# A sigmoid-attention and GELU feed-forward kernel: sixteen SBUF tiles made 32 bytes longer each

## The chip, the cores and the metric

The kernel runs on one core of one Trainium2 chip. The metric is the device time of one execution in microseconds; the time of a version is the median of its runs. TensorE (PE) does the matrix products, ScalarE (ACT) the activations and casts, VectorE (DVE) the subtractions, GpSimd (POOL) a few products early on, SyncE (SP) issues most DMAs. SBUF is the on-chip memory of 128 partitions; an address here is a byte offset within a partition, the same on all partitions of a tile.

## What is computed

```python
scores = q @ k.T / sqrt(64) - log(448)          # 8 batches, 12 heads, 448 positions, head_dim 64
x = (sigmoid(scores) @ v) -> [3584 tokens, 768]
h = x @ w_in                                    # [768, 2048]
g = 0.5 * h * (1 + erf(h / sqrt(2)))            # exact GELU
out = g @ w_out                                 # [2048, 768]
```

The weights come as 64-bit floats. Nearly every matrix product is made of products of a rounded high part and of a low rest (names ending in h and l), in the type fp32r.

## The kernel before

**Work.** The tokens of the eight batches are worked in seven feed-forward passes of T = 512 tokens each (448 of one batch and 64 of another). `attention_first` does the attention of the first two batches and decodes the first weights from 64-bit floats. Then for each pass t, `ffn1(t)` computes the hidden layer, and `window(t + 2, t)` does the second layer of pass t (`ffn2`) with the attention of batch t + 2 woven in between, a few matmuls of one, then a few of the other. The order of instructions on every engine is the order in which the program is written (a manual schedule).

**The g tiles.** There are sixteen of them, one for each block fc of 128 hidden features, tags g0 to g15, made by `g_tile` (line 66). Each has 2 x 512 words of 4 bytes: the high part `g[fc][:, 0]` at its start and the low part `g[fc][:, 1]` 2048 bytes further on. During decoding the same sixteen places first hold the decoded `w_in` (`first_w`, made on line 160, filled by POOL on line 163), which `prepare_to` splits into weights for the first pass (lines 237 and 238) and the SP queue stores to a scratch in HBM (line 201). Afterwards `ffn1` writes g into them: ACT writes the high part (line 466), DVE the low part (line 467).

**Who reads g on PE.** In `ffn2` each of 12 weight units (e, half) has 8 blocks, and each block makes three matmuls into `po`:

```python
nc.tensor.matmul(po, wl, g[fc][:, 0], start=first, stop=False)   # L497
nc.tensor.matmul(po, wh, g[fc][:, 1], start=False, stop=False)   # L498
nc.tensor.matmul(po, wh, g[fc][:, 0], start=False, stop=last)    # L499
```

The second operand after the output is the stationary one (128 columns of weights, 512 bytes of a partition), the third is the moving one (512 columns, 2048 bytes). In all that is 7 x 12 x 8 x 3 = 2016 matmuls, 672 on each of the three lines. `ffn1` makes as many into `ph` (lines 450 to 452) with `xh` and `xl` as moving operands.

**Where the tiles lie.** Tiles lie one behind another in the order of the pools and of first use. The weights `hl` (name `whl`) have four places: for unit number i in `prepare_to`, two buffers of the tag `whl` when i % 4 is 0 or 1 (and in the whole first pass), the buffers of the tags `raw` and `me` when i % 4 is 2 or 3. The first unit of every `ffn2` has i % 4 = 0. The table gives start addresses and their remainders mod 512; a slice of weights lies a multiple of 512 bytes from its tile's start, and so does the low part of a g tile.

| tile | address before | mod 512 | address after | mod 512 |
|---|---|---|---|---|
| xh, xl | 16544, 28832 | 160, 160 | the same | 160, 160 |
| g0 | 41120 | 160 | 41120 | 160 |
| g1 | 45216 | 160 | 45248 | 192 |
| g8 | 73888 | 160 | 74144 | 416 |
| g11 | 86176 | 160 | 86528 | 0 |
| g15 | 102560 | 160 | 103040 | 128 |
| whl in tags raw, me | 117408, 126624 | 160, 160 | 117920, 127136 | 160, 160 |
| qs (three buffers) | 143008, 144800, 146592 | 160, 416, 160 | each 512 more | 160, 416, 160 |
| ka, kb (first buffers) | 148384, 154528 | 416, 416 | each 512 more | 416, 416 |
| whl in tag whl | 211360, 219552 | 416, 416 | 211872, 220064 | 416, 416 |

Of the kernel before, what the change touches and what calls it, by code (L numbers as in the profile page):

```python
# [17 lines left out]
P = 128  # L18
# [4 lines left out]
def tile_sigmoid_attention_gelu_ffn(  # L23
# [25 lines left out]
    T = S + TOK  # L49
# [4 lines left out]
    const = ctx.enter_context(tc.tile_pool(name="const", bufs=1))  # L54
# [7 lines left out]
    xh = const.tile([P, NPAIR, T], F32R, name="xh")  # L62
    xl = const.tile([P, NPAIR, T], F32R, name="xl")
    g, first_w = {}, {}

    def g_tile(fc, name, dtype=F32R):
        return const.tile([P, 2, T], dtype, tag=f"g{fc}", name=name)

    scr_in = tc.dram_tile([NF, P, NC * P], F32, name="scr_in")
    scr_out = tc.dram_tile([NO, P, NFH * P], F32, name="scr_out")  # L70
# [21 lines left out]
    def decoder():  # L92
# [57 lines left out]
        def end(i):  # L150
            high = raws.pop(i)[:, :, 1]
            ended[0] += 1
            m, e = parts.pop(i)
            nc.vector.scalar_tensor_tensor(  # L154
                e, high, 0x80000000, e, op0=ALU.bitwise_and, op1=ALU.bitwise_or
            )
            kind, u, c0, w = chunks[i]
            if c0 == 0 and kind == "in":
                first_w[kind, u] = g_tile(u, f"w_in{u}", F32).rearrange("p a b -> p (a b)")
            elif c0 == 0:  # L160
                first_w[kind, u] = sb.tile([P, WU], F32, tag="wst", name=f"w_out{u}", bufs=WST)
            t = first_w[kind, u][:, c0 : c0 + w]
            nc.gpsimd.tensor_tensor(t, m.bitcast(F32), e.bitcast(F32), op=ALU.mult)  # L163
# [291 lines left out]
    def ffn1(b):  # L455
        for fc in range(NF):
            if b == 0:
                W.store_to(fc + 3)
            if (b, fc) not in phs:
                hidden(b, fc, range(NC - 1))  # L460
            W.prepare_to(W.pos[b, "in", fc] + (2 if b == 0 else AHD))
            ph = hidden(b, fc, range(NC - 1, NC))
            g[fc] = g_tile(fc, f"g{b}_{fc}")
            gf = sb.tile([P, T], F32, tag="tmp", name=f"gf{b}_{fc}", bufs=3)
            nc.scalar.activation(gf, ph, AF.Gelu)  # L465
            nc.scalar.activation(g[fc][:, 0], ph, AF.Gelu)  # L466
            nc.vector.tensor_tensor(g[fc][:, 1], gf, g[fc][:, 0], op=ALU.subtract)  # L467
            W.prepare_to(W.pos[b, "in", fc] + (3 if b == 0 else AHD + 1))
            if fc in (NF - 10, NF - 8):
                load_pair(b + 2, (fc - NF + 10) // 2)  # L470
                load_v(b + 2, (fc - NF + 10) // 2)
            if fc in (NF - 4, NF - 2):
                split_head(b + 2, (fc - NF + 4) // 2)
            if fc == NF - 1:
                load_pair(b + 2, 2)
                load_v(b + 2, 2)
            if b == 0:
                W.decode(PACE_A + PACE_F * min(fc + 1, NF - 1) // (NF - 1))
# [101 lines left out]
```

## Time and profile before

| | |
|---|---|
| median of 3 runs (lowest to highest) | 1275.95 us (1274.27 to 1277.11) |
| the profiled execution: time, span of its trace | 1277.24 us, 1275.5 us |
| busy share of the span: PE, ACT, DVE, POOL | 96%, 68%, 65%, 7% |
| granted TensorE clock, mean over the span | 0.991 of full |

Each instruction in the trace has a start and a duration. Matmuls are pipelined: the next one starts before the one ahead of it ends, so that the distance from start to start, not the duration, is what one costs on PE when they follow each other without a wait. "PEld" rows are loads of the stationary operand, which run beside the matmul ahead.

### The profile page before, as it was taken

Reading aid. Unit: us, or ns where it says so; the run is one execution under the profiler, and the core shown is the slowest. Engines: PE = TensorE matmul, PEld = TensorE weight load, DVE = VectorE, ACT = ScalarE, POOL = GpSimd, SP = SyncE. Lnnn points to the kernel's source line nnn. Section 1 sums busy time; section 2 is a strip of 40 time slices with the busy share of each in tenths; the row PEclk is TensorE's granted clock in tenths of the full one; section 3 lists DMA queues with packets and bytes.
Section 4 is the critical chain, followed back from the end, with each engine's and each line's share of the span. In section 5 each row is a group of like instructions: output and inputs, shape, how many; then the busy total and the mean of one; then the engine's idle time right before and its main releaser. Section 6 shows DMA issues by size and latency. Waiting matters only on the chain.

```text
span 1275.5 us, 15676 instructions
## 1 busy us (share of the span) xinstructions
PE 1229.8 (96%) x5448; PEld 985.9 (77%) x5448; DVE 826.7 (65%) x1359; ACT 872.2 (68%) x1427; POOL 89.1 (7%) x84
## 2 busy tenths in 40 slices
PE   7889888989999999999999999999999999999998
PEld 4445665756888888888888888888888888888887
DVE  5776888883458973479844798436985458863420
ACT  7987677764459984499844898547995469964421
POOL 1111333441000000000000000000000000000000
PEclk9999898999999999999999999999999999999999
DMA  7764756652445323554225442254422444323330
GB/s 284 233 213 127 219 185 191 204 183 88 153 143 168 113 67 102 164 158 149 66 84 167 155 143 70 91 159 150 151 75 82 156 154 139 109 66 99 116 123 34
DMA packets 83775, 176.41 MB, mean 138 GB/s; under 512 B 24432, under 2 KB 37744, under 8 KB 83696
## 3 DMA queue, kind: packets, MB, share of 16 engines
q1 hardware_dynamic: 81968, 169.12, 41.8%
q0 software_dynamic: 1728, 6.29, 1.2%
q8 instruction: 43, 0.70, 0.2%
q14 instruction: 36, 0.29, 0.1%
HBM read 149.03 MB, written 26.35 MB: 137 GB/s over the span
## 4 chain that ended last, share of the span: by engine, by line
PE 80%; DVE 7%; ACT 5%; DMA 2%; issue 2%; POOL 2%; SPq 0%; DVEq 0%; POOLq 0%; ACTq 0%
PE po L497 11%; PE po L498 11%; PE po L499 11%; PE ph L450 10%; PE ph L451 10%; PE ph L452 10%; PE pav L398 7%; PE sc L331 4%; PE sc L332 4%; ACT a L355 2%; PE pav L364 2%; POOL w_out L163 2%; DVE me_ring L154 1%; DVE whl L238 1%; DMA scr_in<-w_in 1%
## 5 line engine op out<-in xcount | busy, mean ns | idle before, releaser
L450 PE MATMUL ph<-xh,whl 128*128 128x512 f32 x672 | 263.9, 393 | 10.3 <-DVE whl L238 10.3
L497 PE MATMUL po<-g,whl 128*128 128x512 f32 x672 | 264.0, 393 | 9.5 <-DVE whl L238 9.5
L498 PE MATMUL po<-g,whl 128*128 128x512 f32 x672 | 262.9, 391 | 0.0
L499 PE MATMUL po<-g,whl 128*128 128x512 f32 x672 | 262.8, 391 | 0.0
L451 PE MATMUL ph<-xl,whl 128*128 128x512 f32 x672 | 262.8, 391 | 0.0
L452 PE MATMUL ph<-xh,whl 128*128 128x512 f32 x672 | 262.6, 391 | 0.0
L238 DVE TENSOR_TENSOR whl<-wst,whl 128x768 fp32r<-128x768 f32 (+1 forms) x168 | 179.5, 1072 | 66.8 <-ACT whl L237 63.6
L467 DVE TENSOR_TENSOR g<-gf,g 128x512 fp32r<-128x512 f32 x112 | 77.8, 695 | 213.2 <-ACT g L466 213.2
L465 ACT ACTIVATE gf<-ph 128x512 f32<-128x512 f32 x112 | 66.8, 597 | 205.1 <-PE ph L452 190.9
L450 PEld LDWEIGHTS ph<-xh,whl 128*128 128x128 f32 x672 | 126.9, 189 | 40.3 <-DVE whl L238 13.3
L237 ACT CAST whl<-wst 128x768 fp32r<-128x768 f32 (+1 forms) x168 | 155.4, 928 | 2.2 <-PE po L499 0.8
L497 PEld LDWEIGHTS po<-g,whl 128*128 128x128 f32 x672 | 126.6, 188 | 38.8 <-DVE whl L238 11.6
L355 ACT ACTIVATE a<-sc 128x896 f32<-128x896 f32 x192 | 129.6, 728 | 28.3 <-PE sc L332 24.0
L499 PEld LDWEIGHTS po<-g,whl 128*128 128x128 f32 x672 | 126.6, 188 | 27.1
L452 PEld LDWEIGHTS ph<-xh,whl 128*128 128x128 f32 x672 | 127.0, 189 | 26.6
L451 PEld LDWEIGHTS ph<-xl,whl 128*128 128x128 f32 x672 | 127.0, 189 | 26.2
L498 PEld LDWEIGHTS po<-g,whl 128*128 128x128 f32 x672 | 126.6, 188 | 23.8
L331 PE MATMUL sc<-qs,ka 128*128 128x448 f32 x288 | 108.6, 377 | 14.9 <-ACT a L355 13.6
L348 DVE TENSOR_TENSOR al<-a,ah 128x896 fp32r<-128x896 f32 x120 | 97.8, 854 | 34.8 <-ACT ah L347 34.8
L332 PE MATMUL sc<-qs,kb 128*128 128x448 f32 x288 | 107.4, 373 | 0.0
L293 DVE TENSOR_TENSOR qs<-qr,qs 64x448 fp32r<-64x448 f32 x96 | 62.0, 646 | 45.8 <-ACT qs L292 43.9
L347 ACT CAST ah<-a 128x896 fp32r<-128x896 f32 x120 | 85.6, 753 | 6.1 <-PE pav L398 4.6
(62 smaller groups left out, 1514.6 us busy)
## 6 DMA issues: line engine op xcount, KB each, us to landing
wst<-scr_in SPq DMA_DIRECT2D x96, 384.0 KB, 3.1
wst<-scr_out SPq DMA_DIRECT2D x72, 512.0 KB, 3.2
kr<-k_dram SPq DMA_DIRECT2D x47, 448.0 KB, 4.4
vr<-v_dram SPq DMA_DIRECT2D x48, 256.0 KB, 3.9
qr<-q_dram SPq DMA_DIRECT2D x48, 224.0 KB, 3.2
out_dram<-ob SPq DMA_DIRECT2D x42, 224.0 KB, 2.0
raw<-w_in_dram SPq DMA_DIRECT2D x20, 384.0 KB, 4.2
scr_in<-w_in SPq DMA_DIRECT2D x16, 384.0 KB, 4.3
```

What stands on the lines that cost most here:

```text
L237: nc.scalar.copy(hl[:, 0, :w], t[:, :w])
L238: nc.vector.tensor_tensor(hl[:, 1, :w], t[:, :w], hl[:, 0, :w], op=ALU.subtract)
L331: nc.tensor.matmul(o, ka[:, keys], qs, start=True, stop=False)
L332: nc.tensor.matmul(o, kb[:, keys], qs, start=False, stop=True)
L348: nc.vector.tensor_tensor(al[t][:, c], a[t][:, c], ah[t][:, c], op=ALU.subtract)
L355: nc.scalar.activation(a, sc, AF.Sigmoid, bias=NEG_LOG_S, scale=SCALE)
L450: nc.tensor.matmul(ph, wl, xh[:, cc], start=cc == 0, stop=False)
L451: nc.tensor.matmul(ph, wh, xl[:, cc], start=False, stop=False)
L452: nc.tensor.matmul(ph, wh, xh[:, cc], start=False, stop=cc == NC - 1)
L497: nc.tensor.matmul(po, wl, g[fc][:, 0], start=first, stop=False)
L498: nc.tensor.matmul(po, wh, g[fc][:, 1], start=False, stop=False)
L499: nc.tensor.matmul(po, wh, g[fc][:, 0], start=False, stop=last)
```

## The change

`g_tile` asks for 8 more words (32 bytes) behind the 2 x 512 of each g tile and hands out a view of the first 2 x 512. Nothing reads or writes the added words.

```diff
     g, first_w = {}, {}
+    PAD = 8
 
     def g_tile(fc, name, dtype=F32R):
-        return const.tile([P, 2, T], dtype, tag=f"g{fc}", name=name)
+        t = const.tile([P, 2 * T + PAD], dtype, tag=f"g{fc}", name=name)
+        return t[:, : 2 * T].rearrange("p (a b) -> p a b", a=2)
```

In the built program every engine has the same instructions with the same waits in the same order as before; line numbers behind the diff are larger by 2. What differs are addresses: g tile n starts 32 n bytes further on, and every tile behind g15 512 bytes further on, as in the table above. Against weights at remainder 416, g0 lies at a distance of 256 mod 512 and g8 now at 0; the other fourteen lie at the fourteen other multiples of 32.

## Rows read from the trace of the kernel before

**Rows 1.** The page's first part: busy time, share of the span and number of instructions of each engine.
```profile
span 1275.5 us, 15676 instructions
PE 1229.8 (96%) x5448; PEld 985.9 (77%) x5448; DVE 826.7 (65%) x1359; ACT 872.2 (68%) x1427; POOL 89.1 (7%) x84
```

**Rows 2.** Stretches of the span: busy time of PE, weight loads, DVE, ACT and POOL in us, each with its number of instructions, then granted clock, DMA share and GB/s.
```profile
180.00:250.00 70.00, 62.62 (x264) 45.17 (x263) 59.25 (x128) 51.21 (x95) 28.74 (x27) 0.95 0.61 189
250.00:350.00 100.00, 93.55 (x417) 68.60 (x416) 56.10 (x106) 54.86 (x94) 22.00 (x19) 1.00 0.44 140
350.00:450.00 100.00, 100.00 (x454) 85.01 (x453) 74.55 (x115) 79.84 (x127) 0.00 (x0) 1.00 0.44 139
600.00:800.00 200.00, 200.00 (x906) 169.89 (x905) 140.55 (x211) 149.76 (x237) 0.00 (x0) 1.00 0.36 115
1000.00:1200.00 200.00, 200.00 (x900) 168.71 (x900) 124.31 (x181) 135.57 (x215) 0.00 (x0) 1.00 0.39 122
```

**Rows 3.** The instructions that touch the g tiles: count, shortest/median/longest duration in ns, first and last start in us.
```profile
L497 PEld LDWEIGHTS po<-g,whl x672: 186/188/330, 195.7 to 1270.4; 128*128 128x128 f32 x168
L497 PE MATMUL po<-g,whl x672: 389/389/795, 195.7 to 1270.6; 128*128 128x512 f32 x168
L498 PE MATMUL po<-g,whl x672: 387/389/628, 196.0 to 1270.9; 128*128 128x512 f32 x168
L499 PE MATMUL po<-g,whl x672: 388/389/628, 196.2 to 1271.1; 128*128 128x512 f32 x168
L466 ACT ACTIVATE g<-ph x112: 586/593/595, 117.2 to 1206.7; 128x512 fp32r<-128x512 f32 x112
L467 DVE TENSOR_TENSOR g<-gf,g x112: 682/692/1122, 117.9 to 1207.3; 128x512 fp32r<-128x512 f32 x112
```

**Rows 4.** PE in order of time, in the second layer of the last pass, start and duration in us: the first matmul of the second layer's unit 0 (weights in the tag whl, remainder 416), of unit 1, of unit 2 (tag raw, remainder 160) and of unit 3 (tag me, remainder 160), with the one behind each.
```profile
1206.03 0.39 PE L497 MATMUL po<-g,whl 128*128 128x512 f32 x1
1206.25 0.39 PE L498 MATMUL po<-g,whl 128*128 128x512 f32 x1
...
1211.46 0.39 PE L497 MATMUL po<-g,whl 128*128 128x512 f32 x1
1211.69 0.39 PE L498 MATMUL po<-g,whl 128*128 128x512 f32 x1
...
1216.90 0.39 PE L497 MATMUL po<-g,whl 128*128 128x512 f32 x1
...
1222.35 0.39 PE L497 MATMUL po<-g,whl 128*128 128x512 f32 x1
```

**Rows 5.** PE and its weight loads in order of time, a little later in the same unit row: start and duration in us.
```profile
1254.98 0.39 PE L497 MATMUL po<-g,whl 128*128 128x512 f32 x1
1254.99 0.19 PEld L498 LDWEIGHTS po<-g,whl 128*128 128x128 f32 x1
1255.21 0.39 PE L498 MATMUL po<-g,whl 128*128 128x512 f32 x1
1255.21 0.19 PEld L499 LDWEIGHTS po<-g,whl 128*128 128x128 f32 x1
```

**Rows 6.** PE in order of time, where seven attention matmuls of 448 columns stand between matmuls that read g.
```profile
620.95 0.36 PE L398 MATMUL pav<-ah,vs 128*128 128x448 f32 x1
...
622.16 0.37 PE L398 MATMUL pav<-ah,vs 128*128 128x448 f32 x1
622.37 0.39 PE L497 MATMUL po<-g,whl 128*128 128x512 f32 x1
622.60 0.40 PE L498 MATMUL po<-g,whl 128*128 128x512 f32 x1
622.83 0.39 PE L499 MATMUL po<-g,whl 128*128 128x512 f32 x1
623.06 0.39 PE L497 MATMUL po<-g,whl 128*128 128x512 f32 x1
623.29 0.39 PE L498 MATMUL po<-g,whl 128*128 128x512 f32 x1
623.51 0.39 PE L499 MATMUL po<-g,whl 128*128 128x512 f32 x1
```

**Rows 7.** The instructions that write qs, whose buffers lie at remainders 160, 416 and 160: shortest/median/longest duration in ns.
```profile
L292 ACT CAST qs<-qr x96: 553/563/568, 3.4 to 1115.3; 64x448 fp32r<-64x448 f32 x96
```

**Rows 8.** The stores of the decoded w_in out of the g tiles' places: issues on the SP queue (ns), and the time from issue to landing in us, shortest/median/longest.
```profile
L201 SPq DMA_DIRECT2D scr_in<-w_in x16: 382/384/999, 106.0 to 171.1; - x16
...
DMA to landing us min/median/max: 3.8/4.3/6.1
```

**Rows 9.** The chain that ended last, in order of time, where it passes through such stores: start and duration in us.
```profile
148.23 5.73 DMA scr_in<-w_in
...
154.55 0.60 DVE g L467
...
158.88 5.76 DMA scr_in<-w_in
...
165.12 0.68 DVE g L467
...
171.12 3.69 DMA scr_in<-w_in
```

## The prediction

> **What bounds the kernel now.** I first read the busy shares of the engines [rows 1]: PE is busy 96% of the span, ACT and DVE two thirds of it, POOL hardly. A busy PE need not be a PE at its best, so the next view is the one by stretches [rows 2]: from 350 us on PE is busy in every microsecond, at a granted clock of 1.00, which is the higher level of 2.4 GHz; before 330 us it waits at times, for decoded weights and their split. So the last three quarters of the span cost as many microseconds as the matmuls take from start to start. In the bound part a change of addresses can act in one way only: on the distance between the starts of two matmuls.
>
> That distance is read in the second layer of the last pass, where nothing is woven in [rows 4]. From the first matmul of unit 0 (1206.03) to that of unit 3 (1222.35) pass 16.32 us, 72 matmuls of 226.7 ns. With 512 columns at one column per cycle of 2.4 GHz a matmul would take 213.3 ns; that PE goes at about one column per cycle shows in the attention matmuls of 448 columns: seven of them take 1.42 us (620.95 to 622.37) [rows 6], 203 ns each, 24 ns less for 64 columns fewer (0.37 ns a column, where a cycle is 0.417). So each matmul of 512 columns pays 226.7 − 213.3 = 13.4 ns, or 32 cycles, that its columns do not explain. The load of the next weights starts 10 ns or less after the matmul that it runs beside and takes 188 ns of its 227 [rows 3, 5], so PE fetches weights and moving columns at the same time, and a collision of the two fetches is one thing these 32 cycles could be. That is the only lever of this change.
>
> **The change, part by part.** It adds, removes and moves no instruction, no wait and no DMA: all counts of the trace stay. What is left are four ways in which an address could have a price.
>
> *1. The 2016 matmuls that read g.* How PE's pace depends on the distance between moving columns and weights, the kernel before has itself tried at two distances: g lies at remainder 160 throughout, the weights of units 0 and 1 at 416 (distance 256), those of units 2 and 3 at 160 (distance 0). Unit 0 takes 5.43 us, unit 1 5.44, unit 2 5.45 [rows 4]: no difference within the 0.01 us of a row, that is within 0.4 ns of a matmul. Durations say the same for the whole run: over 672 matmuls on each line, with both distances among them, shortest and median lie within 2 ns of each other (389 and 389, 387 and 389, 388 and 389) [rows 3], and the longer ones are few. The attention matmuls mix both distances as well. What no row shows is a distance that is not a multiple of 256, and fourteen of the sixteen tiles get one. I bound it from both sides. How many matmuls count: 1728 of the 2016 lie in passes two to seven, where PE is the bound, and 14/16 of them, 1512, get a new distance. Below: all 32 unexplained cycles go, 1512 × 13.4 ns = 20.3 us gained. Above: the nearest rows of a slower pace of the same instructions are the first three g matmuls after a group of attention [rows 6]: 622.37 to 623.06, 0.69 us, 230 ns each, against 226.7; I take it as what a worse meeting of the fetches would cost: 1512 × 3.3 ns = 5.0 us lost. These three rows also speak for the null, as they come after attention matmuls at either distance and end after three, so they follow from what stood before in the queue and not from where g lies. I take 0, by the row nearest to it: two distances half a period apart cost the same to a hundredth of a microsecond in 24 matmuls. A collision that depended on the low bits would have to repeat every 256 bytes or fewer to stay hidden there. There is a reason, too, for none to show at any distance: the moving columns run through 2048 bytes in a matmul and so pass every remainder mod 512 four times, while the weights' 512 bytes are fetched once, wherever both begin.
>
> The Trainium skill, "SBUF — State Buffer", section "Who interferes with whom", says that PE has two independent read ports, one for the moving operand and one for weights, shared with nothing, and that PE never waits on anyone. By that rule the term is 0 at all distances; rows 4 agree for the two they have, and no row here shows the other fourteen.
>
> *2. ACT and DVE writing g, in lines 466 and 467.* A g tile's write by ACT takes 586 to 595 ns in all 112 cases [rows 3], always at remainder 160. What another remainder does to the same engine shows in qs, whose three buffers lie at 160, 416 and 160: 553 to 568 ns over 96 casts [rows 7]. A difference of 2%, 12 ns, on an engine that is busy 75% of the bound stretch [rows 2] is hidden by PE's matmuls; without that cover all 224 instructions at 12 ns would be 2.7 us. I take 0.
>
> *3. The sixteen stores of decoded w_in out of the g tiles' places.* They lie in the first 175 us, where PE is not the bound, and three of them are on the chain that ended last, with 5.73, 5.76 and 3.69 us [rows 9], since g is written to the same place when the store has read it. All sixteen go out from remainder 160 before; after, each from another multiple of 32. Their landing takes 3.8 to 6.1 us at one and the same remainder [rows 8], so the spread has another cause. Ends: the two long ones fall to 3.8 us, −3.9 us; all three rise to 6.1 us, +0.4 + 0.3 + 2.4 = +3.1 us. I take 0, as the sizes and the issue order stay.
>
> *4. Everything else* moves by exactly 512 bytes and keeps its remainder, and it had that freedom before: weights in four places tens of kilobytes apart cost the same [rows 4].
>
> The sum is 0 + 0 + 0 + 0 on the profiled execution's 1277.24 us (span 1275.5 and 1.7 around it); that execution lies 1.3 us above the median of its runs, so the median stays at **1275.95 us**.
>
> **The rivals.** *Faster: the 32 cycles are collisions, and 0 and 256 are both bad distances.* For it: there are unexplained cycles on every matmul, and both distances tried are multiples of 256, so a pattern that repeats each 256 bytes or fewer would show exactly these rows. Against it: the last paragraph of term 1, and the attention matmuls, 448 columns at both distances, pay 203 − 186.7 = 16 ns, more and not less, with seven eighths of the columns. Its time: if all of it goes, 1275.95 − 20.3 = 1255.7 us; if a quarter, 1270.9. It decides from 2.55 / 1512 = 1.7 ns (four cycles) a matmul on.
>
> The Trainium skill, "TensorE: Matmul & The Clock Gate", section "Back-to-back issue gap", gives N/2.4 + 2.5 ns as the gap between back-to-back matmuls with no budget for weight loads, 215.8 ns at 512 columns. By an estimate from that page the most that this rival could gain would be 1512 × (226.7 − 215.8) ns = 16.5 us; no run here shows a pace below 226 ns at 512 columns.
>
> *Slower: a multiple of 256 is the good distance.* For it: rows 6 show that the pace can be worse, in the same instructions at full clock. Against it: that pace ends after three matmuls whatever tile comes. Price: 3.3 ns on 1512 matmuls, 5.0 us, 1281.0 us; the same 1.7 ns a matmul is the point from which it decides, in the places of the second layer from 330 us on.
>
> *The tiles do not lie where the change says.* The table of addresses excludes it: g1 at 192, g11 at 0, weights at 160 and 416.
>
> *The stores turn.* Term 3 gives 1272.1 to 1279.1 us; an end past 2.55 us either way decides.
>
> **How the numbers follow.** A measurement of this kernel tells from no change what exceeds about 0.2%, 2.55 us. No change within that: 0.82. Faster, by collisions that go (0.08) or stores (0.02): 0.10. Slower, by a worse distance (0.06) or stores (0.02): 0.08. The range takes the ends of term 3 (−3.9 and +3.1) and the scatter of the runs before (−1.7 and +1.2): about 1271.0 to 1280.0. That leaves out most of the two PE rivals, 0.12 together.
>
> **What the profile of the changed kernel would show.** Term 1 is right if the units in the last pass still take 5.44 us whatever tile they read and the first start to first start of 24 matmuls doesn't differ between the halves (g0 to g7 and g8 to g15); it is wrong if blocks differ from one another in pace by their tile: then a row by row list of one unit, with sixteen distances, shows which ones. L466 and L467 keep 593 and 692 ns if term 2 holds. In term 3 the landing of scr_in stays at a median of 4.3 us. The forecast is wrong if the distance between starts in `po` leaves 226 to 227 ns while that in `ph`, whose operands keep their remainders, stays.

## The result: 10.0 us slower

The changed kernel takes 1285.99 us (median of 3 runs, 1285.53 to 1286.96) against 1275.95: ratio 1.0081, 95% interval 1.0059 to 1.0104. The forecast was 1275.95 us, no change, with 1271 to 1280 as its range.

The page of the profiled execution after the change (1285.99 us), its first part, and below it the groups of matmuls of both feed-forward layers (busy us, mean ns of one, idle before):

```profile
span 1284.2 us, 15676 instructions
PE 1237.7 (96%) x5448; PEld 983.7 (77%) x5448; DVE 827.6 (64%) x1359; ACT 872.5 (68%) x1427; POOL 89.1 (7%) x84
...
L499 PE MATMUL po<-g,whl 128*128 128x512 f32 x672 | 266.8, 397 | 9.8 <-DVE whl L240 9.8
L452 PE MATMUL ph<-xh,whl 128*128 128x512 f32 x672 | 263.1, 391 | 12.0 <-DVE whl L240 12.0
L501 PE MATMUL po<-g,whl 128*128 128x512 f32 x672 | 265.5, 395 | 0.0
L500 PE MATMUL po<-g,whl 128*128 128x512 f32 x672 | 264.6, 394 | 0.0
```

For ph and for the first matmuls on g, L452 and L499, the page of the kernel before has:

```profile
L450 PE MATMUL ph<-xh,whl 128*128 128x512 f32 x672 | 263.9, 393 | 10.3 <-DVE whl L238 10.3
L497 PE MATMUL po<-g,whl 128*128 128x512 f32 x672 | 264.0, 393 | 9.5 <-DVE whl L238 9.5
```

The counts are those of [rows 1]. The matmuls that read g have become longer (391 to 393 ns in the mean before, 394 to 397 now), those that read xh have not. (Lines are larger by 2: L499 to L501 are lines 497 to 499 of before, L452 is L450.) The same two stretches of 200 us as in [rows 2], PE busy in all of both and the clock at 1.00:

```profile
600.00:800.00 200.00, 200.00 (x897) 167.91 (x896) 139.18 (x208) 148.90 (x235) 0.00 (x0) 1.00 0.35 113
1000.00:1200.00 200.00, 200.00 (x893) 167.32 (x892) 124.30 (x181) 133.69 (x212) 0.00 (x0) 1.00 0.36 118
```

In the same time PE gets through 897 and 893 matmuls, where it had been 906 and 900. It waits for nobody more than before; each matmul costs more. How much is read in the last pass, by the start of one unit of 24 matmuls to the start of the next, as in [rows 4]:

```profile
1218.65 0.40 PE L499 MATMUL po<-g,whl 128*128 128x512 f32 x1
...
1224.23 0.40 PE L499 MATMUL po<-g,whl 128*128 128x512 f32 x1
...
1229.81 0.40 PE L499 MATMUL po<-g,whl 128*128 128x512 f32 x1
```

5.58 us a unit, 232.5 ns a matmul, in place of 226.7. That 1728 matmuls of passes two to seven times 5.8 ns make 10.0 us, as much as the whole loss, is in part chance, since the last pass has no attention between its matmuls. Adding up all distances from start to start in the trace from pass two on shows where the loss lies: the matmuls into po go from 227.65 to 232.57 ns in the mean (+8.5 us), the 840 attention matmuls of 448 columns from 202.7 to 204.1 (+1.2 us, though none of their own distances between moving operand and weights changed), those into ph from 226.67 to 226.80 (+0.2 us); together +9.9 us.

The other terms stayed. Writing g, and storing w_in (issues by line, KB, median us to landing):

```profile
L468 ACT ACTIVATE g<-ph x112: 586/593/595, 115.3 to 1213.8; 128x512 fp32r<-128x512 f32 x112
L469 DVE TENSOR_TENSOR g<-gf,g x112: 683/693/1122, 115.9 to 1214.4; 128x512 fp32r<-128x512 f32 x112
```
```profile
scr_in<-w_in SPq DMA_DIRECT2D x16, 384.0 KB, 4.4
```

They are the values of [rows 3] and [rows 8] to a nanosecond and to 0.1 us.

### The profile page after: what moved, and what is told of

The parts are those of the page before. It is cut to its first block, busy times and chain, and to the rows that moved or that the text cites. A ratio compares the mean times of both kernels' runs of the same rounds, so it can differ in the third digit from the quotient of the medians.

```text
span 1284.2 us, 15676 instructions
## 1 busy us (share of the span) xinstructions
PE 1237.7 (96%) x5448; PEld 983.7 (77%) x5448; DVE 827.6 (64%) x1359; ACT 872.5 (68%) x1427; POOL 89.1 (7%) x84
## 3 DMA queue, kind: packets, MB, share of 16 engines
q0 software_dynamic: 1728, 6.29, 1.2%
## 4 chain that ended last, share of the span: by engine, by line
PE 82%; DVE 7%; ACT 6%; issue 2%; POOL 2%; DMA 2%; SPq 0%; DVEq 0%; POOLq 0%; ACTq 0%
PE po L499 11%; PE po L501 11%; PE po L500 11%; PE ph L452 10%; PE ph L453 10%; PE ph L454 10%; PE pav L400 7%; PE sc L333 4%; PE sc L334 4%; PE pav L366 3%; ACT a L357 2%; DVE whl L240 2%; POOL w_out L165 1%; DVE me_ring L156 1%; PE sc_l L329 1%
## 5 line engine op out<-in xcount | busy, mean ns | idle before, releaser
L499 PE MATMUL po<-g,whl 128*128 128x512 f32 x672 | 266.8, 397 | 9.8 <-DVE whl L240 9.8
L452 PE MATMUL ph<-xh,whl 128*128 128x512 f32 x672 | 263.1, 391 | 12.0 <-DVE whl L240 12.0
L501 PE MATMUL po<-g,whl 128*128 128x512 f32 x672 | 265.5, 395 | 0.0
L469 DVE TENSOR_TENSOR g<-gf,g 128x512 fp32r<-128x512 f32 x112 | 77.8, 695 | 213.3 <-ACT g L468 213.3
L452 PEld LDWEIGHTS ph<-xh,whl 128*128 128x128 f32 x672 | 126.5, 188 | 41.9 <-DVE whl L240 14.9
L499 PEld LDWEIGHTS po<-g,whl 128*128 128x128 f32 x672 | 126.1, 188 | 41.9 <-DVE whl L240 12.2
L501 PEld LDWEIGHTS po<-g,whl 128*128 128x128 f32 x672 | 126.2, 188 | 30.4
```

Source lines behind the costliest of these rows:

```text
L452: nc.tensor.matmul(ph, wl, xh[:, cc], start=cc == 0, stop=False)
```

## Which address counts: four kernels that move tiles as a whole

Three theories fit a loss in po alone. **Distance**: the start of the moving operand minus that of the weights sets PE's pace. **Step**: a moving operand that begins at another remainder than the one ahead costs extra, as in the changed kernel from each g tile to the next. **Start**: g's own remainder counts, wherever the weights lie. All four kernels are the kernel before with tiles moved by 32 bytes, and nothing else. A ratio from here on is against the kernel before as run again in the same set: its median was 1275.83 us beside these four, 1275.81 and 1276.56 us beside later ones.

**g alone, all sixteen alike**

```diff
-    xl = const.tile([P, NPAIR, T], F32R, name="xl")
+    xl_long = const.tile([P, NPAIR * T + 8], F32R, name="xl")
+    xl = xl_long[:, : NPAIR * T].rearrange("p (a b) -> p a b", a=NPAIR)
...
-        return const.tile([P, 2, T], dtype, tag=f"g{fc}", name=name)
+        pad = 120 if fc == NF - 1 else 0
+        t = const.tile([P, 2 * T + pad], dtype, tag=f"g{fc}", name=name)
+        return t[:, : 2 * T].rearrange("p (a b) -> p a b", a=2)
```

> All sixteen g tiles lie 32 bytes further on than before, at one common remainder (192 mod 512), everything behind them 512 further on; so g stands at a distance of 32 or 288 from the weights in every matmul, and successive g tiles have the same remainder. Distance theory (the remainder of moving operand minus weights sets the pace of a matmul): the 24 matmuls of a unit in the last pass leave 5.44 us, towards the 5.58 of the change, and the time goes from 1276 towards 1286 us. Step theory (a moving operand that begins at another remainder than the one ahead of it costs extra, a lasting remainder does not): 5.44 us a unit, 1276 us within 1.5. Start theory (g's own remainder matters, whatever the weights'): like distance, away from 5.44 us.

Measured 1288.51 us, ratio 1.0102 (1.0085 to 1.0119). Units of the last pass:

```profile
1220.69 0.39 PE L500 MATMUL po<-g,whl 128*128 128x512 f32 x1
...
1226.29 0.39 PE L500 MATMUL po<-g,whl 128*128 128x512 f32 x1
```

5.60 us, 233.3 ns a matmul, with no step between tiles anywhere. The step theory falls.

**Everything behind g, the weights too; g, xh and xl stay**

```diff
-        return const.tile([P, 2, T], dtype, tag=f"g{fc}", name=name)
+        pad = 8 if fc == NF - 1 else 0
+        t = const.tile([P, 2 * T + pad], dtype, tag=f"g{fc}", name=name)
+        return t[:, : 2 * T].rearrange("p (a b) -> p a b", a=2)
```

> g, xh and xl stay at remainder 160, everything behind them, the weights too, moves by 32 bytes (weights at 192 and 448). Distance theory: the pace of both layers (po and ph) leaves 226.7 ns, up to twice the change's loss, so up to 1296 us. Step theory: 226.7 ns in both, 1276 us. Start theory: 226.7 ns in both, as g and xh lie where they lay; at most the attention matmuls change.

Measured 1298.25 us, ratio 1.0172 (1.0156 to 1.0188). Now both layers are slow, po and ph, by their groups on the page:

```profile
L452 PE MATMUL ph<-xh,whl 128*128 128x512 f32 x672 | 267.3, 398 | 10.7 <-DVE whl L240 10.7
L499 PE MATMUL po<-g,whl 128*128 128x512 f32 x672 | 267.4, 398 | 8.2 <-DVE whl L240 8.2
```

The moving operands had not moved by a byte. The start theory falls, and the loss is twice that of the change (+22 us), since twice as many matmuls have a new distance.

**Everything**

```diff
-    one = const.tile([P, 8], F32, name="one")[:, :1]
+    one = const.tile([P, 16], F32, name="one")[:, :1]
```

> Every tile moves by 32 bytes, so all distances stay and all remainders change by 32. Distance theory and step theory: 226.7 ns in both layers, 1276 us. Start theory: ph and po both leave 226.7 ns, up to 1296 us.

Measured 1276.45 us, ratio 1.0006 (0.9996 to 1.0015): all remainders new, all distances old, no change. This also excludes that the weights' own start counts, which the run before had left open. The stretch of 600 to 800 us has the 906 matmuls of [rows 2] again:

```profile
600.00:800.00 200.00, 200.00 (x906) 169.79 (x905) 140.25 (x210) 149.78 (x237) 0.00 (x0) 1.00 0.36 114
```

**g8 to g15 alone**

```diff
+        pad = {7: 8, NF - 1: 120}.get(fc, 0)
```

(in the place of the pad of the first of these kernels, without the longer xl)

> g0 to g7 at remainder 160 as before, g8 to g15 at 192; one step of 32 between two units of the second layer, none inside a unit. Distance theory: every second unit of the last pass (the odd ones, which read g8 to g15) leaves 5.44 us, half the change's loss, about 1281 us. Step theory: 5.44 us plus at most some 0.02 us in the three matmuls behind the step, 84 steps of it, so 1276 to 1278 us. Start theory: like distance.

Measured 1283.07 us, ratio 1.0056 (1.0040 to 1.0071). Units 0 to 3 of the last pass, of which the odd ones read g8 to g15:

```profile
1209.99 0.39 PE L499 MATMUL po<-g,whl 128*128 128x512 f32 x1
...
1215.43 0.40 PE L499 MATMUL po<-g,whl 128*128 128x512 f32 x1
...
1221.03 0.40 PE L499 MATMUL po<-g,whl 128*128 128x512 f32 x1
...
1226.51 0.40 PE L499 MATMUL po<-g,whl 128*128 128x512 f32 x1
```

5.44, 5.60 and 5.48 us: the slow units are those with the distance of 32, in the same run, on the same engine, with no attention woven in. The 0.04 us that unit 2 has over unit 0 lies in its first seven distances (1.624 us, where seven at 226.7 ns are 1.587); the later ones are 226 and 227 ns, so the matmuls right behind a slow unit still pay.

So it is the distance. [rows 4] fit with a pattern that repeats every 256 bytes, as 0 and 256 cost the same there; the second of the kernels that follow shows that it does.

## The pace at each distance, PE alone

A kernel of PE matmuls with next to nothing beside them, weights at one place, the moving operand 4 bytes further in each series (this kernel and the three others of this kind further on were run once each):

```python
for s, (n, o, m, count) in enumerate(SEGMENTS):      # 64 series: n = 512, o = 0 .. 63, m = 128, count = 48
    for i in range(count):
        nc.tensor.matmul(po[:m, :n], wx[:, :m], wx[:, 512 + o : 512 + o + n], ...)
```

> A kernel that leaves out the whole computation of the reference: PE alone makes 64 series of 48 matmuls (128 columns of weights, 512 moving columns, fp32r), in each series with the moving operand 4 bytes further from the weights: distances 0, 4, ... 252 mod 256. Distance theory: 226.7 ns from start to start in the series at distance 0 and about 233.3 at 32, as in the whole kernel; between them either a step (any distance but 0 slow) or a slope. Rival, that the slower pace needs the other engines' traffic in SBUF (ACT, DVE and DMA rest here): 226.7 ns or less in all series. Open on purpose: whether a distance goes below 226.7.

The last 24 matmuls of six series (distance 0, 28, 32, 64, 132 and 240 bytes), each from the start of one matmul to the start of the 24th behind it; a window's count has one or two more, cut at its ends:

```profile
40.07:45.51 5.44, 5.44 (x26) 4.51 (x25) 0.00 (x0) 0.00 (x0) 0.00 (x0) 1.00 0.00 0
118.33:123.77 5.44, 5.44 (x26) 4.50 (x25) 0.00 (x0) 0.00 (x0) 0.00 (x0) 1.00 0.01 3
129.36:134.96 5.60, 5.60 (x26) 4.50 (x24) 0.00 (x0) 0.00 (x0) 0.00 (x0) 1.00 0.00 0
218.43:223.92 5.49, 5.49 (x26) 4.51 (x24) 0.00 (x0) 0.00 (x0) 0.00 (x0) 1.00 0.00 0
408.56:414.32 5.76, 5.76 (x26) 4.62 (x24) 0.00 (x0) 0.00 (x0) 0.00 (x0) 1.00 0.00 0
711.01:716.45 5.44, 5.44 (x26) 4.51 (x25) 0.00 (x0) 0.00 (x0) 0.00 (x0) 1.00 0.01 3
```

With DVE, ACT and the DMA queues at rest, distance 32 costs the same 233.3 ns as in the whole kernel: no other engine is needed for it. The pace lies between 226.7 ns (at 0, 28, 60, 156, 236, 240, 252 bytes) and 240.0 (at 20, 132, 196, 244); 233.3 is the commonest. In cycles of 2.4 GHz that is 512 and 32 to 64 more; 226.7 is the least of all 64 distances. At the eight multiples of 32, which are the distances of the change:

| distance mod 256 | 0 | 32 | 64 | 96 | 128 | 160 | 192 | 224 |
|---|---|---|---|---|---|---|---|---|
| ns from start to start | 226.67 | 233.33 | 228.88 | 233.29 | 233.33 | 234.29 | 233.33 | 233.38 |

Their mean is 232.06; the changed kernel, which goes through all eight once in each unit, has 232.5 in the last pass. So the price of the change can be had from this table within about 1 us: (232.06 − 226.67) x 1728 = 9.3 us, where po lost 8.5 and the whole kernel 10.0.

**Sizes**

```python
SEGMENTS = ...  # n = 128 .. 512, o = 0 .. 264, m = 32 .. 128, in the loop above
```

> The computation is left out as in the kernel of single distances; series of 48 matmuls with 448 moving columns at distances 0, 16, ... 240, with 512 columns at distances 256, 288, ... 512 and 1024, with 128 to 384 columns at distances 0, 32, 64 and 128, and with 32, 64 and 96 columns of weights at 512 moving columns. Distance theory with a period of 256 bytes: 256, 512 and 1024 give 226.7 ns, 288 to 480 give what 32 to 224 give. If PE's extra time comes from weight reads that stand in the way of moving reads, fewer columns of weights cost fewer extra cycles (32 of 128 at distance 0, so about 16 at 64 columns), whatever the number of moving columns; if it is a fixed price of changing weights, it stays at 32 cycles for all.

The last 24 matmuls of six series: 512 columns at a distance of 256 and of 288, 256 columns at 0 and at 32, and at distance 0 512 columns with 64 and at distance 128 with 96 columns of weights:

```profile
194.94:200.38 5.44, 5.44 (x26) 4.50 (x25) 0.00 (x0) 0.00 (x0) 0.00 (x0) 1.00 0.00 0
205.97:211.57 5.60, 5.60 (x26) 4.50 (x25) 0.00 (x0) 0.00 (x0) 0.00 (x0) 1.00 0.00 0
357.44:360.32 2.88, 2.88 (x27) 2.88 (x26) 0.00 (x0) 0.00 (x0) 0.00 (x0) 1.00 0.00 0
363.15:365.98 2.83, 2.83 (x27) 2.83 (x26) 0.00 (x0) 0.00 (x0) 0.00 (x0) 1.00 0.02 6
488.81:494.33 5.52, 5.52 (x25) 3.22 (x24) 0.00 (x0) 0.00 (x0) 0.00 (x0) 1.00 0.00 0
566.42:571.98 5.56, 5.56 (x25) 3.88 (x24) 0.00 (x0) 0.00 (x0) 0.00 (x0) 1.00 0.00 0
```

Distances of 256, 512 and 1024 gave 226.67 ns, 288 and 1056 gave 233.33 like 32, 320 gave 228.88 like 64: the period is 256 bytes. With 384 moving columns the pace is 173.33 ns at 0, 32 and 64 and 176.08 at 128; with 320 it is 146.67 at all four, with 128 and 192 it is 111.67 at all four. With 256 columns distance 0 is the slowest of the four: 120.00 ns, against 117.75 at 32, 117.79 at 64 and 118.67 at 128. With 448 columns it goes from 200.00 (at 16, 64, 160) through 202.67 (at 0, where the kernel before has its attention) to 206.67 (at 112, 144). So of the lengths tried the distance counts at 256 columns and from 384 on, and which distance is the best depends on their length. The 32 cycles that 226.7 ns has over its columns are there at distance 0 with 256, 320, 384 and 512 columns alike (with 448 it is 38), and fewer columns of weights don't lessen them: at distance 0, 96 and 64 columns of weights gave 230.0 ns, 32 gave 231.67, all slower than 128. A price per weight column that the moving columns pay is thereby excluded for these 32 cycles; what they are is open. For the part that the distance adds it is not excluded: at a distance of 128, 96, 64 and 32 columns of weights gave 231.67, 229.33 and 230.25 ns, less than the 233.33 of 128.

## How far that map carries

**g moved by 64 bytes** (the first kernel's diff with 16 and 112 for 8 and 120)

> As where g was moved by 32 bytes, but by 64: distance 64 mod 256 in the second layer. If the series of single distances hold in the whole kernel at multiples of 32: 228.9 ns, 5.49 us a unit, 2.2 ns on 1728 matmuls, 1279.8 us. Rival, that any distance other than 0 mod 256 costs the same 6.7 ns here: 5.60 us a unit, 1287 us.

Measured 1281.41 us, ratio 1.0041 (1.0027 to 1.0055). Two units of the last pass:

```profile
1214.88 0.39 PE L500 MATMUL po<-g,whl 128*128 128x512 f32 x1
...
1220.38 0.39 PE L500 MATMUL po<-g,whl 128*128 128x512 f32 x1
```

5.50 us, 229 ns, as in the table. At 32 and 64 bytes, the two multiples of 32 to which g was moved as a whole, the map holds in the whole kernel; over passes two to seven po has 230.1 ns in the mean, as groups of attention interrupt the series.

**Weights moved by 16 bytes, and by 60**

```diff
-                hl = sb.tile([P, 2, WU], F32R, tag=tag, name=f"whl{i}", bufs=bufs)
+                hl = sb.tile([P, 2 * WU + 64], F32R, tag=tag, name=f"whl{i}", bufs=bufs)
+                hl = hl[:, 4 : 4 + 2 * WU].rearrange("p (a b) -> p a b", a=2)
```

(15 in the place of 4 in the second)

> The split weights begin 16 bytes later in their places (each place 256 bytes longer), g, xh and xl as before: distance 240 mod 256 for all matmuls of both layers. In the series of single distances 240 had 226.67 ns, like 0, with 224 at 233.4 and 244 at 240.0 beside it. If those series hold in the whole kernel: 5.44 us a unit, 1276 us within 1.5. Rival, that in the whole kernel only a distance of 0 is good: about 233 ns in both layers, 1298 us, as where the weights were moved by 32.

> The same with 60 bytes: distance 196 mod 256 for all matmuls of both layers, which had 240.0 ns in the series, the most of all. If the series hold: 5.76 us a unit, 13.33 ns more on the 3456 matmuls of passes two to seven, 46 us, so about 1322 us. Rival, that any distance other than the good one costs the same 6.7 ns: 1298 us.

Measured 1296.49 us (1.0164, 1.0149 to 1.0179) and 1296.74 us (1.0163, 1.0146 to 1.0180). Both have 5.60 us a unit, 233.3 ns; here the first:

```profile
1229.27 0.39 PE L498 MATMUL po<-g,whl 128*128 128x512 f32 x1
...
1234.87 0.39 PE L498 MATMUL po<-g,whl 128*128 128x512 f32 x1
```

Both expectations of the map fell: 240 was not good and 196 was not the worst. Either the distance alone is not enough below 32 bytes, or what stands ahead matters. A further kernel tried both, with the weights moved in the place of the moving operand, and with 1, 2, 3 or 7 matmuls of 448 columns ahead of a series.

```python
SEGMENTS = [(0, 0, 0), (0, 0, 0)] + [(0, o, 0) for o in range(64)]
SEGMENTS += [(o, 0, k) for o in range(0, 64, 8) for k in (1, 2, 3, 7)]
```

> The computation is left out: series of 48 matmuls of 512 columns, 64 of them with the weights (not the moving operand) 0, 4, ... 252 bytes further on, then 32 with the moving operand 0, 32, ... 224 further and 1, 2, 3 or 7 matmuls of 448 columns ahead. If the distance alone set the pace down to 4 bytes, weights moved by 16 and 60 would give what the moving operand moved by 240 and 196 gave, 226.7 and 240.0 ns; if the two operands count each for itself below 32 bytes, they give 233.3 as in the whole kernel. If the pace has one value at each multiple of 32, the matmuls ahead change nothing (226.7 at 0, 233.3 at 32, 228.9 at 64, 234.3 at 160); if what stands ahead chooses among several lasting paces, they differ between 1, 2, 3 and 7.

The last 24 matmuls of four series: weights moved by 16, weights moved by 60, and the moving operand at 64 with one and with two matmuls of 448 columns ahead:

```profile
82.58:88.18 5.60, 5.60 (x26) 4.54 (x24) 0.00 (x0) 0.00 (x0) 0.00 (x0) 1.00 0.02 3
205.55:211.07 5.52, 5.52 (x26) 4.50 (x24) 0.00 (x0) 0.00 (x0) 0.00 (x0) 1.00 0.01 3
845.32:850.92 5.60, 5.60 (x26) 4.54 (x25) 0.00 (x0) 0.00 (x0) 0.00 (x0) 1.00 0.00 0
856.84:862.34 5.50, 5.50 (x26) 4.51 (x25) 0.00 (x0) 0.00 (x0) 0.00 (x0) 1.00 0.01 3
```

Weights moved by 16 give 233.3 ns, as in the whole kernel, where a moving operand moved by 240 gave 226.7. Over all 64 places the two ways to one distance (weights forward, or the moving operand) agree within 0.2 ns at the eight multiples of 32, and at 43 of the 56 others they differ by more than 1 ns. So off the multiples of 32 the distance alone does not set the pace. That below 32 bytes each operand counts for itself is the likelier reason, as weights moved by 16 give 233.3 ns in the whole kernel too, behind quite other matmuls; but it is not shown apart from what stands ahead, as the series ahead was another one in the two kernels. And what stands ahead does count: one distance can have more than one lasting pace, for at 64 bytes it is 233.3 behind one matmul of 448 columns and 228.9 behind two, three or seven; at 128 bytes 233.3 and 232.1 to 232.7. At 0, 32, 96, 160, 192 and 224 what stands ahead changes nothing beyond 0.3 ns. Weights moved by 60 gave 230.0 in the series and 233.3 in the whole kernel; that difference is not explained.

## A faster version

In the kernel before, the attention's 448-column matmuls stand at distance 0, which is not their best, and the first three g matmuls behind each group of seven pay 230 ns [rows 6]. A series copied this alternation, 12 matmuls of 512 columns at distance 0 and 7 of 448 with one operand moved by 0, 4, ... 252 bytes.

```python
for i in range(12):
    nc.tensor.matmul(po, wx[:, :128], wx[:, 512:1024], ...)
for i in range(7):
    nc.tensor.matmul(pa[:, :448], wx[:, 128 + ow : 256 + ow], wx[:, 1088 + om : 1536 + om], ...)
```

> The computation is left out: groups of 12 matmuls of 512 columns at distance 0 and 7 of 448 columns, as second layer and attention alternate in the whole kernel; in 64 series the moving operand of the 448 lies 0, 4, ... 252 bytes further, in 64 more their weights do. At distance 0, as in the kernel before, seven take about 1.42 us. If each matmul keeps the pace that it has in a long series, distances 16, 64 and 160 give 1.40 us for seven (200.0 ns) and leave the 512 at 226.7; if what stands ahead decides, groups as short as seven show no such gain.

Twelve and then seven matmuls, at distance 0, with the moving operand of the seven at 64, and with it at 140 bytes:

```profile
27.49:30.22 2.73, 2.73 (x13) 2.25 (x12) 0.00 (x0) 0.00 (x0) 0.00 (x0) 1.00 0.00 0
30.22:31.64 1.42, 1.42 (x8) 1.31 (x7) 0.00 (x0) 0.00 (x0) 0.00 (x0) 1.00 0.00 0
227.75:230.52 2.77, 2.77 (x13) 2.25 (x12) 0.00 (x0) 0.00 (x0) 0.00 (x0) 1.00 0.00 0
230.52:231.93 1.41, 1.41 (x9) 1.31 (x7) 0.00 (x0) 0.00 (x0) 0.00 (x0) 1.00 0.00 0
465.67:468.39 2.72, 2.72 (x14) 2.25 (x12) 0.00 (x0) 0.00 (x0) 0.00 (x0) 1.00 0.00 0
468.39:469.79 1.40, 1.40 (x9) 1.31 (x7) 0.00 (x0) 0.00 (x0) 0.00 (x0) 1.00 0.00 0
```

At distance 0 twelve and seven took 2.735 and 1.419 us; seven take 1.42 in the whole kernel [rows 6]. What stands ahead counts here: the twelve never moved, and yet took 2.719 to 2.783 us by the place of the seven. Of the three distances that were best in long series, 64 and 160 came out slower in all (4.173 and 4.180 us against 4.154) and 16 no faster (4.154). But others gained on both sides: with the moving operand at 136, 140 or 188 bytes the two took 2.719 and 1.401 us, 4.120 in all; with the weights at 188, 2.724 and 1.409. These places were found by trying, not worked out from a cause. So qs was moved by 140 and vs by 188:

```diff
-        qs = sb.tile([P, S], F32R, tag="qs", name=f"qs{b}_{h}", bufs=3)
+        qs = sb.tile([P, S + 64], F32R, tag="qs", name=f"qs{b}_{h}", bufs=3)[:, 35 : 35 + S]
...
-            vs = sb.tile([P, 2, 4, 2 * D], F32R, tag="vs", name=f"vs{b}_{hp}")
+            vs = sb.tile([P, 16 * D + 64], F32R, tag="vs", name=f"vs{b}_{hp}")
+            vs = vs[:, 47 : 47 + 16 * D].rearrange("p (j c d) -> p j c d", j=2, c=4)
```

> g, xh, xl and the split weights of both layers as before; of the attention's operands qs (moving) lies 140 bytes further in its place and vs (weights) 188, each place 256 bytes longer. In the mixed series these gave 4.12 and 4.13 us for 12 matmuls of the second layer and 7 of the attention, against 4.15 at distance 0. If that holds here, 120 such groups gain about 0.034 and 0.021 us by turns, 3.3 us in all: 1272.5 us, faster than the kernel before by 0.26%. Rival, that the fine map of 4-byte shifts does not carry over (as 240 and 196 did not): 1276 us or more.

Measured 1272.60 us against 1276.56 for the kernel before: ratio 0.9965 (0.9954 to 0.9976), faster than the kernel before, 4 us where 3.3 were worked out. The place that answers to [rows 6]:

```profile
618.55 0.36 PE L399 MATMUL pav<-ah,vs 128*128 128x448 f32 x1
...
619.96 0.39 PE L498 MATMUL po<-g,whl 128*128 128x512 f32 x1
620.19 0.39 PE L499 MATMUL po<-g,whl 128*128 128x512 f32 x1
620.41 0.39 PE L500 MATMUL po<-g,whl 128*128 128x512 f32 x1
620.64 0.39 PE L498 MATMUL po<-g,whl 128*128 128x512 f32 x1
```

Seven attention matmuls take 1.41 us, and the three g matmuls behind them 0.68 us in place of 0.69. Over passes two to seven po goes from 227.65 to 226.78 ns (−1.5 us), the scores from 202.7 to 200.1 (−1.1 us), the values from 202.7 to 201.3 (−0.6 us), together −3.2 us; the rest of the 4 is within the runs' scatter (1270.82 to 1273.17 us, and 1274.29 to 1278.01 before).

## Why the prediction was wrong, step by step

- **What bounds the kernel, and by what quantity: right.** It said that in the bound part a change of addresses can act only on the distance from start to start, and 9.9 of the 10.0 us came there.
- **Term 1, the matmuls that read g: wrong, and it decided.** "I take 0, by the row nearest to it" went from two distances to all. But the two were one: 0 and 256 are the same distance in the pattern of 256 bytes that the runs showed. The text had named that gap itself ("a pattern that repeats each 256 bytes or fewer would show exactly these rows") and then closed it with an argument: "There is a reason, too, for none to show at any distance: the moving columns run through 2048 bytes in a matmul and so pass every remainder mod 512 four times". That is the step that failed. Distance 32 costs 233.3 ns and distance 0 226.7, with the same bytes passed.
- **The rule that the prediction leaned on does not hold for the time here.** Weights moved by 32 bytes cost 6.7 ns on each matmul of both layers in the last pass and in `ffn1`. The Trainium skill, "SBUF — State Buffer", section "Who interferes with whom", by which PE's two read ports are independent and PE never waits, would give 0 at all distances. The runs show that the two operands' addresses matter together; they do not show that a port is shared.
- **The price of the slower rival was too small.** "a multiple of 256 is the good distance" is what the runs show at 512 columns, and it had a chance of 0.06. It was priced by [rows 6] at 3.3 ns on 1512 matmuls, 5.0 us. Over passes two to seven po lost 4.9 ns on all 1728, 8.5 us (two of the sixteen tiles keep a good distance, but not the good pace: in the last pass the three matmuls on g8, behind slow ones, take 234, 229 and 231 ns), and the other matmuls 1.4 us, for which the price had nothing. The end of the range on that side, 1280.0, came from the stores and the scatter and did not take this rival in. (Added up, its two parts give 1270.4 to 1280.3.)
- **The reading of [rows 6] was half right.** They do follow from what stood ahead; but they also belong to addresses, since the slower pace vanishes when the attention's operands are moved (0.68 us for three).
- **The faster rival: not borne out.** Of 64 distances none went below 226.6 ns at 512 columns. What the 32 cycles at distance 0 are stays open.
- **Terms 2 and 3: right.** L468 and L469 kept their durations, and the stores' landing had a median of 4.4 us, where it had been 4.3.
- **Term 4: right for ph, not for the attention.** ph went from 226.67 to 226.80 ns. The attention's matmuls kept every remainder and yet lost 1.2 us in all: their pace depends on the matmuls between which they stand, and the term had no place for that.
- **What would show it wrong** was named rightly: po left 226 to 227 ns, ph did not.

## What to carry to other kernels

Where PE is the bound with long fp32r matmuls, the start address of the moving operand minus that of the weights, mod 256 bytes, is a tuning parameter worth some per cent of PE's time: with one operand moved, 512 moving columns took 226.7 to 240.0 ns in a series of their own. For 512 columns keep all operands at distances of 0 mod 256 as a start. That does not carry over to every length: at 256 columns 0 was the slowest of four distances, at 448 it was not the best of sixteen. The series are of fp32r; no other type was run. After any edit that changes a tile's length compare the distance from start to start, not the busy share, which stayed at 96%. When a trace shows the same time at two values of a parameter, ask what period would make the two one value before going on to all the others.

## What was not expected

- A matmul's pace on PE has states that last: at one distance (64 bytes) a series ran at 228.9 or at 233.3 ns depending on whether one or two matmuls of 448 columns stood ahead of it. Behind a group of 448 columns it takes three matmuls to settle [rows 6], behind a unit at another distance seven.
- Lasting paces often lie at whole steps of 8 cycles: 544, 552, 560, 568 and 576 cycles (226.7, 230.0, 233.3, 236.7, 240.0 ns) for 512 columns. What the steps are is open.
- Fewer columns of weights made a matmul of 512 columns slower at distance 0: 230.0 ns with 64 or 96, 231.7 with 32, 226.7 with 128. At a distance of 128 bytes it was the other way round.
